# Scores with the query stationary, and packed by column tile, in a decode attention kernel

## Chip, cores and metric

The kernel runs on one core of a Trainium2 chip. The metric is device time in microseconds (us) of one execution; lower is better. A kernel's time is the median of several executions. A program on one core has no second core to compare with, so "fast" here only means that a run lies within 1.5% of the fastest of the same kernel.

PE is the matmul engine (PEld its weight loads), DVE the vector engine, ACT the scalar engine, POOL the general engine, SP the engine that issues the DMAs. "The Trainium skill" is a set of notes on the chip, named by page title and section.

## The reference, cut to what matters

One token of a decoder block: layer norm, attention over a long cache, and a small feed-forward block. Nearly all the data is the cache.

```python
x: (1, 1, 448)   Hq, Hkv, Sk, Dh = 16, 8, 32768, 256        # all bf16
k_cache, v_cache: (1, 8, 32768, 256)                        # 134 MB each
scores = einsum("bhqd,bhkd->bhqk", q, k) * Dh**-0.5         # 2 query heads share a K/V head
p = softmax(scores, axis=-1)
o = einsum("bhqk,bhkd->bhqd", p, v)
h = x + o @ wo;   h2 = h + FFN(layernorm(h))                # FFN: 448 -> 1792 -> 448, Mish
```

K and V together are 268.4 MB. The other weights are about 10 MB.

## The kernel before

The cache is read in chunks of 4096 rows (2 MiB): 8 chunks of K and 8 of V for each of 8 K/V heads ("groups"). Chunks share six rotating SBUF buffers. While the K chunks of group g come in, so do the V chunks of group g−1. K is transposed on PE, two bf16 at a time as one f32; the copy out of PSUM is called an eviction here.

```python
    for b in range(NB):                                   # k_chunk: 8 batches of 4 slabs of 128 rows
        pst = ps_t.tile([P, 4, P], F32, ...)
        for jj in range(4):
            nc.tensor.transpose(out=pst[:, jj, :], in_=kn[:, j, :].bitcast(F32), identity=ident_f[:])
        kT = ktp.tile([P, 4, P, 2], BF16, ...)            # evicted by ACT (3 of 8) or DVE (5 of 8)
        ...
        for jj in range(4):
            for e in range(2):                            # kT is the weight, q (2 columns padded to 16) moves
                nc.tensor.matmul(out=pss[:, j, :], lhsT=kT[:, jj, :, e], rhs=qT_pad[:, g, e, :], ...)
    # ... softmax_group: DVE max, POOL all-reduce of the max, two exps on ACT, sum by a matmul
    # v_chunk: 16 matmuls of 512 columns in four column tiles
            nc.tensor.matmul(out=acc[32 * t:32 * t + 2 * REP, reg, :], lhsT=pT[:, slab:slab + 2, :]...,
                             rhs=vn[:, j:j + 2, :]..., tile_position=(0, 32 * t))
```

The tile pools are laid out in SBUF in the order in which they are opened: first small constants, then small work tiles, then the six stream buffers:

```python
    const = ctx.enter_context(tc.tile_pool(name="const", bufs=1))
    small = ctx.enter_context(tc.tile_pool(name="small", bufs=2))
    stream = ctx.enter_context(tc.tile_pool(name="stream", bufs=STREAM_BUFS))   # kn and vn
```

So every byte in `const` and `small` moves the buffers into which K and V land.

## Time and profile before

| | before |
|---|---|
| median, fastest, slowest of the first 5 runs | 683.9, 683.62, 684.43 us |
| profiled span | 682.2 us |
| K/V transfers | 128 of 2 MiB |
| share of the span that the 16 DMA engines were busy with queue q1 | 97.4% |
| PE / DVE / ACT busy | 81% / 38% / 31% |

The first fence is from the page of the kernel before: busy time by engine, then rows of 40 equal slices of the span (a digit is a busy share in tenths, the last row is what the DMA engines moved), then the DMA queues with packets, MB, and the time of their packets as a share of 16 engines' span.

```profile
PE 549.6 (81%) x7643; PEld 418.6 (61%) x7643; DVE 256.3 (38%) x475; ACT 208.7 (31%) x231; POOL 11.8 (2%) x29
...
DMA  8999999999999999999999999999999999999981
GB/s 282 399 427 425 427 422 413 427 426 422 426 424 429 424 427 426 427 425 426 426 426 428 426 425 428 425 427 426 423 427 428 424 426 427 428 424 426 428 366 61
...
q1 hardware_dynamic: 22090, 279.00, 97.4%
q8 instruction: 60, 0.98, 0.6%
```

The DMA engines never rest, and the rate sits near 426 GB/s from the third slice to the 38th. That is the bound. Besides the data, the same engines carry 60 packets of 16 KiB that bring instructions.

The second fence is from the groups of instructions of the kernel before: line, engine, operation, tiles, shapes, count; then busy us and mean ns; then the idle time before them and what ended it.

```profile
L209 PE MATMUL pst<-ident_f,kn 128*128 128x128 f32 x2048 | 353.3, 306 | 44.2 <-DMA kn<-in_A_k_cache_dram 44.2
L215 DVE COPY kT<-pst 128x512 f32<-128x512 f32 x320 | 221.0, 691 | 290.4 <-PE pst L209 288.9
L212 ACT COPY kT<-pst 128x1024 bf16<-128x1024 bf16 x192 | 194.2, 1011 | 398.3 <-PE pst L209 393.2
L220 PE MATMUL pss<-qT_pad,kT 128*128 128x16 bf16 x4096 | 184.0, 172 | 22.7 <-DVE kT L215 17.0
L255 PE MATMUL acc<-vn,pT 128*4 128x512 bf16 x1024 | 101.9, 422 | 14.4 <-DMA vn<-in_A_v_cache_dram 14.4
```

PE waits for K data (44.2 us in front of the transposes), not the data for PE. The P·V matmuls (L255) last 422 ns each but cover 101.9 us in all, 100 ns each: about four overlap.

### The profile page before, as it was taken

To read this page: it belongs to the slowest core of one execution; us is meant where nothing else is said; L and a number is where in the kernel's file an instruction comes from. 1 tells how busy PE (TensorE), PEld (TensorE's weight loads), DVE (VectorE), ACT (ScalarE), POOL (GpSimd) and SP (SyncE) were. 2 spreads that over 40 slices of the span, in tenths; PEclk is the share of its full clock that TensorE was granted. 3 is DMA by queue.
4 is the path that set the end of the run, shared out by engine and by line. 5 is a ranking of instruction groups with operands and counts; after the bars stand their busy time and mean duration, and the time that the engine had idled before them with its cause. 6 is when DMAs were issued, how large, how long until landed. Compare 5 with 4: busy or idle time off the path is not lost.

```text
span 682.2 us, 16927 instructions
## 1 busy us (share of the span) xinstructions
PE 549.6 (81%) x7643; PEld 418.6 (61%) x7643; DVE 256.3 (38%) x475; ACT 208.7 (31%) x231; POOL 11.8 (2%) x29
## 2 busy tenths in 40 slices
PE   2869979987998897888887789888988979877345
PEld 2757756666765775666566666567656757665114
DVE  1335624442443443343433334334433334434002
ACT  0324443332332342232332234222332323322101
POOL 2100000000000000000000000000000000000000
PEclk9969979997998888987998789877899889889655
DMA  8999999999999999999999999999999999999981
GB/s 282 399 427 425 427 422 413 427 426 422 426 424 429 424 427 426 427 425 426 426 426 428 426 425 428 425 427 426 423 427 428 424 426 427 428 424 426 428 366 61
DMA packets 22164, 280.08 MB, mean 411 GB/s; under 512 B 2186, under 2 KB 4235, under 8 KB 5580
## 3 DMA queue, kind: packets, MB, share of 16 engines
q1 hardware_dynamic: 22090, 279.00, 97.4%
q8 instruction: 60, 0.98, 0.6%
q14 instruction: 12, 0.10, 0.0%
q10 hardware_dynamic: 2, 0.00, 0.0%
HBM read 278.99 MB, written 0.00 MB: 409 GB/s over the span
## 4 chain that ended last, share of the span: by engine, by line
DMA 41%; PE 38%; issue 9%; DVE 5%; ACT 4%; POOLq 1%; POOL 1%; SPq 0%; ACTq 0%; DVEq 0%
DMA kn<-in_A_k_cache_dram 36%; PE pst L209 20%; PE pss L220 10%; PE acc L255 6%; DMA vn<-in_A_v_cache_dram 3%; DVE kT L215 3%; ACT kT L212 3%; DMA wq_sb<-in_A_wq_dram 2%; POOLq L367 1%; ACT pT L236 1%; DVE m L228 1%; PE psm L162 1%; PE psm L310 1%; POOL mall L230 0%; DVE S L222 0%
## 5 line engine op out<-in xcount | busy, mean ns | idle before, releaser
L209 PE MATMUL pst<-ident_f,kn 128*128 128x128 f32 x2048 | 353.3, 306 | 44.2 <-DMA kn<-in_A_k_cache_dram 44.2
L215 DVE COPY kT<-pst 128x512 f32<-128x512 f32 x320 | 221.0, 691 | 290.4 <-PE pst L209 288.9
L212 ACT COPY kT<-pst 128x1024 bf16<-128x1024 bf16 x192 | 194.2, 1011 | 398.3 <-PE pst L209 393.2
L209 PEld LDWEIGHTS pst<-ident_f,kn 128*128 128x128 f32 x2048 | 246.9, 155 | 68.8 <-issue 45.4
L220 PEld LDWEIGHTS <-kT 128*128 128x128 bf16 x4096 | 156.6, 99 | 98.7 <-DVE kT L215 51.4
L220 PE MATMUL pss<-qT_pad,kT 128*128 128x16 bf16 x4096 | 184.0, 172 | 22.7 <-DVE kT L215 17.0
L255 PE MATMUL acc<-vn,pT 128*4 128x512 bf16 x1024 | 101.9, 422 | 14.4 <-DMA vn<-in_A_v_cache_dram 14.4
L255 PEld LDWEIGHTS <-pT 128*4 128x4 bf16 x1024 | 20.2, 85 | 37.4 <-issue 33.7
L222 DVE COPY S<-pss 128x64 f32<-128x64 f32 x64 | 14.4, 224 | 44.5 <-PE pss L220 44.5
L239 PE MATMUL psm<-L,ones_f 128*128 128x2 f32 x16 | 3.7, 300 | 21.0 <-ACT pT L236 20.9
L239 PEld LDWEIGHTS psm<-L,ones_f 128*128 128x128 f32 x16 | 3.0, 234 | 22.6 <-ACT pT L236 22.6
L236 ACT ACTIVATE pT<-S,negM 128x256 bf16<-128x256 f32 x16 | 8.8, 575 | 23.3 <-POOL negM L231 22.8
L264 DVE COPY accn<-acc 128x512 f32<-128x512 f32 x8 | 5.5, 682 | 27.7 <-PE acc L255 27.7
L267 PE MATMUL psm<-sel,accn 128*128 128x2 f32 x32 | 7.0, 287 | 9.0 <-DVE accn L264 9.0
L267 PEld LDWEIGHTS psm<-sel,accn 128*128 128x128 f32 x32 | 5.9, 229 | 13.4 <-DVE accn L264 13.4
L141 ACT ACTIVATE rstd_ln<-psm,eps_t 128x1 f32<-128x1 f32 x2 | 0.5, 261 | 42.4 <-PE psm L139 42.4
L230 POOL PARTITION_ALL_REDUCE mall<-m x8 | 3.0, 376 | 540.5 <-DVE m L228 540.5
L241 DVE RECIPROCAL rl<-psm 128x2 f32<-128x2 f32 x8 | 1.3, 169 | 20.3 <-PE psm L239 20.3
L280 PEld LDWEIGHTS <-wo_flat 128*128 128x128 bf16 x128 | 5.5, 108 | 3.0 <-issue 3.0
L269 PE MATMUL psm<-sel,accn 128*128 128x2 f32 x32 | 7.1, 292 | 0.0
L162 PE MATMUL psm<-cenbf_ln,wq_sb 128*128 128x1 bf16 x128 | 3.7, 165 | 3.7 <-DMA wq_sb<-in_A_wq_dram 3.3
L280 PE MATMUL psm<-oT,wo_flat 128*128 128x1 bf16 x128 | 4.4, 164 | 2.5 <-DVE oT L273 2.5
(71 smaller groups left out, 61.3 us busy)
## 6 DMA issues: line engine op xcount, KB each, us to landing
kn<-in_A_k_cache_dram SPq DMA_DIRECT2D x64, 2048.0 KB, 21.8
vn<-in_A_v_cache_dram SPq DMA_DIRECT2D x64, 2048.0 KB, 24.5
wo_flat<-in_A_wo_dram SPq DMA_DIRECT2D x1, 3584.0 KB
wq_sb<-in_A_wq_dram SPq DMA_DIRECT2D x2, 1536.0 KB, 9.4
w_flat<-in_B_w_dram SPq DMA_DIRECT2D x1, 1568.0 KB, 30.0
w_sb<-in_B_w_dram SPq DMA_DIRECT2D x1, 1344.0 KB, 26.8
wq_sb<-in_A_wq_dram SPq DMA_DIRECT2D x2, 256.0 KB, 11.8
w_sb<-in_B_w_dram SPq DMA_DIRECT2D x1, 224.0 KB
```

Of the source, the lines that this page charges most:

```text
L162: nc.tensor.matmul(out=psm[:, PM_Q + fb:PM_Q + fb + 1], lhsT=wq_sb[:, c, h * DH:(h + 1) * DH].rearrange("p (i e) -> p e i", e=2)[:, e, :], ...
L209: nc.tensor.transpose(out=pst[:, jj, :], in_=kn[:, j, :].bitcast(F32), identity=ident_f[:])
L212: nc.scalar.copy(out=kT[:].rearrange("p a r e -> p (a r e)"), in_=pst[:].rearrange("p a r -> p (a r)").bitcast(BF16))
L215: nc.vector.tensor_copy(out=kT[:].rearrange("p a r e -> p (a r e)").bitcast(F32), in_=pst[:].rearrange("p a r -> p (a r)"))
L220: nc.tensor.matmul(out=pss[:, j, :], lhsT=kT[:, jj, :, e], rhs=qT_pad[:, g, e, :], start=(e == 0), stop=(e == 1))
L222: nc.vector.tensor_copy(out=S_sb[:, c * J:(c + 1) * J, :], in_=pss[:, :, 0:REP])
L228: nc.vector.tensor_reduce(out=m1[:], in_=view, axis=AX.X, op=ALU.max)
L236: nc.scalar.activation(out=pT[:, :, hh], in_=view[:, hh, :], func=ACT.Exp, bias=negM[:, h:h + 1], scale=SCALE, accum_out=L1[:, h:h + 1])
L255: nc.tensor.matmul(out=acc[32 * t:32 * t + 2 * REP, reg, :], lhsT=pT[:, slab:slab + 2, :].rearrange("p s h -> p (s h)"), rhs=vn[:, j:j + 2 ...
L267: nc.tensor.matmul(out=psm[:, PM_OT + dc * REP:PM_OT + (dc + 1) * REP], lhsT=accv[:, 0, dc, :], rhs=sel32[:, 0:REP], start=True, stop=False)
L269: nc.tensor.matmul(out=psm[:, PM_OT + dc * REP:PM_OT + (dc + 1) * REP], lhsT=accv[:, 1, dc, :], rhs=sel32[:, REP:2 * REP], start=False, st ...
L280: nc.tensor.matmul(out=psm[:, PM_ATT + nb:PM_ATT + nb + 1], lhsT=wo_flat[:, col * D + nb * P:col * D + (nb + 1) * P], rhs=oT[:, dc, hh:hh ...
```

## The change

Intent: take work off PE. The scores are turned round, so that q (two columns) is the weight and 512 K positions move, four column tiles at once: 16 matmuls a chunk instead of 64. The scores come out as rows (each of the four column tiles fills two partitions, one a query head, so 8 of 128 partitions carry scores), so they must be transposed back before P·V (8 small transposes a chunk). Evictions are split evenly between ACT and DVE, ACT copies 512 f32 instead of 1024 bf16, and the softmax sum is now combined over the partitions by POOL, as the maximum was before.

```diff
-EVAC_ON_ACT = (False, True, False, False, True, False, True, False)
+EVAC_ON_ACT = (False, True, False, True, False, True, False, True)
-KT_BUFS = 8
+KT_BUFS = 7
...
-    ones_f = const.tile([P, P], F32, name="ones_f")
...
-    b1_row = const.tile([1, FF], BF16, name="b1_row")          # moves to the pool of wq, behind the stream
...
-            for jj in range(4):
-                for e in range(2):
-                    nc.tensor.matmul(out=pss[:, j, :], lhsT=kT[:, jj, :, e], rhs=qT_pad[:, g, e, :],
-                                     start=(e == 0), stop=(e == 1))
-        nc.vector.tensor_copy(out=S_sb[:, c * J:(c + 1) * J, :], in_=pss[:, :, 0:REP])
+            for e in range(2):
+                for t in range(4):
+                    kT = kTs[bg * 4 + t]
+                    nc.tensor.matmul(out=bank[32 * t:32 * t + REP, :], lhsT=qT2[:, g, e, :],
+                                     rhs=kT[:, :, :, e], start=(e == 0), stop=(e == 1),
+                                     tile_position=(0, 32 * t))
+            nc.vector.tensor_scalar(out=S1[:, col0:col0 + 512], in0=bank[:], scalar1=1.0, scalar2=None,
+                                    op0=ALU.mult, op1=ALU.max, accum_out=rmax[:, idx:idx + 1])
...
+        for c in range(NCH):                                    # softmax_exp, once a group
+            nc.scalar.activation(out=S1[:, c * CCOLS:(c + 1) * CCOLS], ..., func=ACT.Exp, ...)
...
+        for blk in range(NB):                                   # p_transpose, once a chunk
+            nc.tensor.transpose(out=ppt[:, blk, :], in_=S1[:, col0:col0 + P], identity=ident_bf[:])
```

Which transfers are issued, in which order, and into how many buffers, does not change. (Cuts in the code are marked with three dots; the comments in the diffs are mine.) In the compiled program the six stream buffers start at byte 29376 of each partition (and every 16384 behind it) before, and at 25344 after. PE has 13181 instructions before and 8083 after.

More of the change, by code (lines that the diff above doesn't have):

```diff
@@ L16 @@
 P = 128
-EVAC_ON_ACT = (False, True, False, False, True, False, True, False)
+EVAC_ON_ACT = (False, True, False, True, False, True, False, True)
+S_EVAC_ON_ACT = (False, False)
 J_SLABS = 32
 STREAM_BUFS = 6
-KT_BUFS = 8
-S_PAD = 16
-PV_TILES = 4
+KT_BUFS = 7
+S_LAG = 2
+NEG_BIG = -3.0e38
 @with_exitstack
@@ L54 @@
     J = J_SLABS
+    assert J == 32
     CH = J * P
     NCH = SK // CH
-    assert SK % CH == 0 and J % 4 == 0
-    NCJ = NCH * J
+    assert SK % CH == 0
     SCALE = float(DH) ** -0.5
@@ L61 @@
     NB = J // 4
+    NHALF = 2
+    CCOLS = NHALF * 512
+    NCOLS = NCH * CCOLS
     const = ctx.enter_context(tc.tile_pool(name="const", bufs=1))
@@ L66 @@
     ktp = ctx.enter_context(tc.tile_pool(name="ktp", bufs=KT_BUFS))
+    s1p = ctx.enter_context(tc.tile_pool(name="s1p", bufs=2))
     ptp = ctx.enter_context(tc.tile_pool(name="ptp", bufs=2))
-    ssp = ctx.enter_context(tc.tile_pool(name="ssp", bufs=2))
     ps_t = ctx.enter_context(tc.tile_pool(name="ps_t", bufs=3, space=bass.MemoryType.PSUM))
-    ps_s = ctx.enter_context(tc.tile_pool(name="ps_s", bufs=2, space=bass.MemoryType.PSUM))
+    ps_s = ctx.enter_context(tc.tile_pool(name="ps_s", bufs=1, space=bass.MemoryType.PSUM))
+    ps_p = ctx.enter_context(tc.tile_pool(name="ps_p", bufs=1, space=bass.MemoryType.PSUM))
     ps_a = ctx.enter_context(tc.tile_pool(name="ps_a", bufs=1, space=bass.MemoryType.PSUM))
@@ L77 @@
     make_identity(nc, ident_f[:])
-    ones_f = const.tile([P, P], F32, name="ones_f")
-    nc.vector.memset(ones_f[:], 1.0)
     onesD = const.tile([P, P], F32, name="onesD")
@@ L90 @@
     nc.vector.tensor_reduce(out=sel32[:], in_=ident_f[:].rearrange("p (t q) -> p q t", q=32), axis=AX.X, op=ALU.add)
+    sel2 = sel32[:, 0:REP]
+    selneg2 = const.tile([P, REP], F32, name="selneg2")
+    nc.vector.tensor_scalar(out=selneg2[:], in0=sel2, scalar1=-SCALE, scalar2=None, op0=ALU.mult)
+    negbig2 = const.tile([P, REP], F32, name="negbig2")
+    nc.vector.tensor_scalar(out=negbig2[:], in0=sel2, scalar1=-NEG_BIG, scalar2=NEG_BIG, op0=ALU.mult, op1=ALU.add)
     psm = ps_m.tile([P, 512], F32, name="psm")
-    acc = ps_a.tile([P, 2, 2 * DH], F32, name="acc")
+    acc = ps_a.tile([P, 2 * DH], F32, name="acc")
     nc.vector.memset(acc[:], 0.0)
+    pss = [ps_s.tile([P, 512], F32, name=f"pss{i}") for i in range(2)]
+    for i in range(2):
+        nc.vector.memset(pss[i][:], 0.0)
     PM_X = 0
@@ L98 @@
     PM_VAR = 8
-    PM_L = 10
     PM_OT = 12
@@ L110 @@
     nc.sync.dma_start(out=x_row[0:1, 0:D], in_=A_x[0, 0:1, :])
-    b1_row = const.tile([1, FF], BF16, name="b1_row")
-    nc.sync.dma_start(out=b1_row[0:1, :], in_=B_b1.rearrange("(o f) -> o f", o=1))
     wq_pool = tc.tile_pool(name="wq", bufs=1)
     wqp = wq_pool.__enter__()
+    b1_row = wqp.tile([1, FF], BF16, name="b1_row")
+    nc.sync.dma_start(out=b1_row[0:1, :], in_=B_b1.rearrange("(o f) -> o f", o=1))
     wq_sb = wqp.tile([P, NDC, HQ * DH], BF16, name="wq_sb")
@@ L164 @@
                                  rhs=cen1_bf[:, c:c + 1], start=(c == 0), stop=(c == NDC - 1))
-    qT_pad = const.tile([P, HKV, 2, S_PAD], BF16, name="qT_pad")
-    nc.gpsimd.memset(qT_pad[:], 0.0)
-    nc.vector.tensor_scalar(out=qT_pad[:, :, :, 0:REP].rearrange("p g e hh -> p g hh e"),
+    qT2 = const.tile([P, HKV, 2, REP], BF16, name="qT2")
+    nc.vector.tensor_scalar(out=qT2[:].rearrange("p g e hh -> p g hh e"),
                             in0=psm[:, PM_Q:PM_Q + NFB].rearrange("p (g hh e) -> p g hh e", g=HKV, hh=REP),
@@ L187, in load_ffn_weights, with flush_pending @@
         nc.sync.dma_start(out=w2_flat[:, 0:NFC * D], in_=B_w2.rearrange("(p fc) n -> p (fc n)", p=P))
-    L1 = const.tile([P, HQ], F32, name="L1")
-    negM = const.tile([P, HQ], F32, name="negM")
-    rl = const.tile([P, HQ], F32, name="rl")
     attn_sb = const.tile([P, NDC], F32, name="attn_sb")
     nc.vector.memset(attn_sb[:], 0.0)
-    S_tiles = {}
+    S1_tiles = {}
+    rmax_tiles = {}
     pT_tiles = {}
+    rl_tiles = {}
+    sbank = [0]
+    pending = []
+    def flush_pending():
+        while pending:
+            pending.pop(0)()
     def k_chunk(g, c):
@@ L201, in k_chunk, with scores @@
         if c == 0:
-            S_tiles[g] = ssp.tile([P, NCJ, REP], F32, name=f"S_{g}", tag="S")
-        S_sb = S_tiles[g]
-        pss = ps_s.tile([P, J, S_PAD], F32, name=f"pss_{g}_{c}", tag="pss")
+            S1_tiles[g] = s1p.tile([P, NCOLS], BF16, name=f"S1_{g}", tag="S1")
+            rmax_tiles[g] = small.tile([P, NCH * NHALF], F32, name=f"rmax_{g}", tag="rmax")
+        S1 = S1_tiles[g]
+        rmax = rmax_tiles[g]
+        kTs = {}
+        def scores(bg):
+            bank = pss[sbank[0] % 2]
+            sbank[0] += 1
+            for e in range(2):
[4 more added lines that the diff above has]
+                                     tile_position=(0, 32 * t))
+            col0 = (c * NHALF + bg) * 512
+            idx = c * NHALF + bg
+            nc.vector.tensor_scalar(out=S1[:, col0:col0 + 512], in0=bank[:], scalar1=1.0, scalar2=None,
+                                    op0=ALU.mult, op1=ALU.max, accum_out=rmax[:, idx:idx + 1])
         for b in range(NB):
@@ L211, in k_chunk @@
             if EVAC_ON_ACT[b % 8]:
-                nc.scalar.copy(out=kT[:].rearrange("p a r e -> p (a r e)"),
-                               in_=pst[:].rearrange("p a r -> p (a r)").bitcast(BF16))
+                nc.scalar.copy(out=kT[:].rearrange("p a r e -> p (a r e)").bitcast(F32),
+                               in_=pst[:].rearrange("p a r -> p (a r)"))
             else:
@@ L216, in k_chunk @@
                                       in_=pst[:].rearrange("p a r -> p (a r)"))
-            for jj in range(4):
-                j = b * 4 + jj
-                for e in range(2):
-                    nc.tensor.matmul(out=pss[:, j, :], lhsT=kT[:, jj, :, e], rhs=qT_pad[:, g, e, :],
-                                     start=(e == 0), stop=(e == 1))
-        nc.vector.tensor_copy(out=S_sb[:, c * J:(c + 1) * J, :], in_=pss[:, :, 0:REP])
-    def softmax_group(g):
-        S_sb = S_tiles.pop(g)
-        view = S_sb[:].rearrange("p cj hh -> p hh cj")
-        m1 = small.tile([P, REP], F32, name=f"m1_{g}", tag="m1")
-        nc.vector.tensor_reduce(out=m1[:], in_=view, axis=AX.X, op=ALU.max)
-        mall = small.tile([P, REP], F32, name=f"mall_{g}", tag="mall")
-        nc.gpsimd.partition_all_reduce(out_ap=mall[:], in_ap=m1[:], channels=P, reduce_op=ReduceOp.max)
-        nc.gpsimd.tensor_scalar(out=negM[:, g * REP:(g + 1) * REP], in0=mall[:], scalar1=-SCALE, scalar2=None,
-                                op0=ALU.mult)
-        pT = ptp.tile([P, NCJ, REP], BF16, name=f"pT_{g}", tag="pT")
-        for hh in range(REP):
-            h = g * REP + hh
-            nc.scalar.activation(out=pT[:, :, hh], in_=view[:, hh, :], func=ACT.Exp, bias=negM[:, h:h + 1],
-                                 scale=SCALE, accum_out=L1[:, h:h + 1])
-        pT_tiles[g] = pT
-        nc.tensor.matmul(out=psm[:, PM_L:PM_L + REP], lhsT=ones_f[:], rhs=L1[:, g * REP:(g + 1) * REP],
-                         start=True, stop=True)
-        nc.vector.reciprocal(out=rl[:, g * REP:(g + 1) * REP], in_=psm[:, PM_L:PM_L + REP])
@@ new lines, in k_chunk, with softmax_stats @@
+            kTs[b] = kT
+            if b == S_LAG - 1:
+                flush_pending()
+            if b - S_LAG == 3:
+                scores(0)
+        pending.append(lambda: scores(1))
+    def softmax_stats(g):
+        rmax = rmax_tiles.pop(g)
+        rowmax = small.tile([P, 1], F32, name=f"rowmax_{g}", tag="rowmax")
+        nc.vector.tensor_reduce(out=rowmax[:], in_=rmax[:], axis=AX.X, op=ALU.max)
+        m2 = small.tile([P, REP], F32, name=f"m2_{g}", tag="m2")
+        nc.vector.scalar_tensor_tensor(out=m2[:], in0=sel2, scalar=rowmax[:, 0:1], in1=negbig2[:],
+                                       op0=ALU.mult, op1=ALU.add)
+        mall = small.tile([P, REP], F32, name=f"mall_{g}", tag="mall")
+        nc.gpsimd.partition_all_reduce(out_ap=mall[:], in_ap=m2[:], channels=P, reduce_op=ReduceOp.max)
+        junk2 = small.tile([P, REP], F32, name=f"junk2_{g}", tag="junk2")
+        negM_row = small.tile([P, 1], F32, name=f"negM_{g}", tag="negM")
+        nc.vector.scalar_tensor_tensor(out=junk2[:], in0=mall[:], scalar=1.0, in1=selneg2[:],
+                                       op0=ALU.mult, op1=ALU.mult, accum_out=negM_row[:])
+        return negM_row
@@ new lines, in softmax_exp @@
+    def softmax_exp(g, negM_row):
+        S1 = S1_tiles[g]
+        lrow = small.tile([P, NCH], F32, name=f"lrow_{g}", tag="lrow")
+        for c in range(NCH):
+            nc.scalar.activation(out=S1[:, c * CCOLS:(c + 1) * CCOLS], in_=S1[:, c * CCOLS:(c + 1) * CCOLS],
+                                 func=ACT.Exp, bias=negM_row[:, 0:1], scale=SCALE, accum_out=lrow[:, c:c + 1])
+        lsum = small.tile([P, 1], F32, name=f"lsum_{g}", tag="lsum")
+        nc.vector.tensor_reduce(out=lsum[:], in_=lrow[:], axis=AX.X, op=ALU.add)
+        l2 = small.tile([P, REP], F32, name=f"l2_{g}", tag="l2")
+        nc.vector.tensor_scalar(out=l2[:], in0=sel2, scalar1=lsum[:, 0:1], scalar2=None, op0=ALU.mult)
+        lall = small.tile([P, REP], F32, name=f"lall_{g}", tag="lall")
+        nc.gpsimd.partition_all_reduce(out_ap=lall[:], in_ap=l2[:], channels=P, reduce_op=ReduceOp.add)
+        rl = small.tile([P, REP], F32, name=f"rl_{g}", tag="rl")
+        nc.vector.reciprocal(out=rl[:], in_=lall[:])
+        rl_tiles[g] = rl
+        pT_tiles[g] = ptp.tile([P, NCH, J, REP], BF16, name=f"pT_{g}", tag="pT")
@@ new lines, in p_transpose @@
+    def p_transpose(g, c):
+        S1 = S1_tiles[g]
+        pT = pT_tiles[g]
+        ppt = ps_p.tile([P, NB, P], BF16, name=f"ppt_{g}_{c}", tag="ppt")
+        for blk in range(NB):
+            col0 = c * CCOLS + blk * P
+            nc.tensor.transpose(out=ppt[:, blk, :], in_=S1[:, col0:col0 + P], identity=ident_bf[:])
+        for bg in range(NHALF):
+            nc.vector.tensor_copy(
+                out=pT[:, c, bg * 16:(bg + 1) * 16, :].rearrange("p (t jj) hh -> p jj t hh", t=4),
+                in_=ppt[:, bg * 4:(bg + 1) * 4, :].rearrange("p jj (t q) -> p jj t q", q=32)[:, :, :, 0:REP])
@@ L245, in v_chunk @@
         nc.sync.dma_start(out=vn[:], in_=A_v_cache[0, g, c * CH:(c + 1) * CH, :].rearrange("(r j) d -> r j d", j=J))
+        if c + 1 < NCH:
+            p_transpose(g, c + 1)
         pT = pT_tiles[g]
-        reg = g % 2
         NPAIR = J // 2
         for pi in range(NPAIR):
-            t = pi % PV_TILES
+            t = pi % 4
             j = 2 * pi
-            slab = c * J + j
-            first = (c == 0 and pi < PV_TILES)
-            last = (c == NCH - 1 and pi >= NPAIR - PV_TILES)
-            nc.tensor.matmul(out=acc[32 * t:32 * t + 2 * REP, reg, :],
-                             lhsT=pT[:, slab:slab + 2, :].rearrange("p s h -> p (s h)"),
+            first = (c == 0 and pi < 4)
+            last = (c == NCH - 1 and pi >= NPAIR - 4)
+            nc.tensor.matmul(out=acc[32 * t:32 * t + 2 * REP, :],
+                             lhsT=pT[:, c, j:j + 2, :].rearrange("p s h -> p (s h)"),
                              rhs=vn[:, j:j + 2, :].rearrange("p a d -> p (a d)"),
@@ L261, in finish_group @@
         pT_tiles.pop(g)
-        reg = g % 2
+        S1_tiles.pop(g)
+        rl = rl_tiles.pop(g)
         accn = small.tile([P, 2 * DH], F32, name=f"accn_{g}", tag="accn")
-        nc.vector.tensor_copy(out=accn[:], in_=acc[:, reg, :])
+        nc.vector.tensor_copy(out=accn[:], in_=acc[:])
         accv = accn[:].rearrange("p (s i e) -> p s e i", s=2, e=2)
@@ L273, in finish_group @@
             nc.vector.tensor_tensor(out=oT[:, dc, :], in0=psm[:, PM_OT + dc * REP:PM_OT + (dc + 1) * REP],
-                                    in1=rl[:, g * REP:(g + 1) * REP], op=ALU.mult)
+                                    in1=rl[:], op=ALU.mult)
         for nb in range(NDC):
@@ L287, in finish_group, with softmax_group @@
                                 in1=attn_sb[0:DLAST, NDC - 1:NDC], op=ALU.add)
+    def softmax_group(g):
+        flush_pending()
+        negM_row = softmax_stats(g)
+        softmax_exp(g, negM_row)
+        p_transpose(g, 0)
     for c in range(NCH):
```

## The prediction

> **What bounds the kernel now.** The K and V stream. Every 8 us stretch from 40 to 656 us moves 417 to 432 GB/s with the DMA engines fully busy, except 96 to 112 us (404 and 414; windows view). The DMA table: 128 transfers of 2 MiB, q1 97.4% of 16 engines. One transfer lasts 2.097 MB / 426 GB/s = 4.92 us, so a K/V pair takes 9.85 us. With a backlog PE does a pair in 7.85 us (timeline, 112.5 to 120.4 us), then waits for K data (44 us in all, groups view), and the queue is about 22 us ahead of it (issue to landing 21.8 us). After the last V chunk lands (663.8 us) a serial tail of 18.4 us follows.
>
> **What the change removes, adds and moves.**
> - Scores: 4096 matmuls with kT stationary (184.0 us in all, 2.9 us a chunk) become 16 matmuls a chunk of 512 columns with two query columns stationary, in four column tiles. The 1024 P·V matmuls have that form already: mean 422 ns, but they cover only 101.9 us, 0.1 us each. So I estimate 1.6 us a chunk. The Trainium skill, "TensorE: Matmul & The Clock Gate", Part 3, says that matmuls in different column tiles run concurrently; this trace agrees (422 against 100 ns).
> - ACT evictions: 3 of 1011 ns a chunk become 4 on 512 f32 elements, an estimated 0.6 us each.
> - DVE a chunk: 5 copies of 0.69 us + 0.22 become 4 × 0.69, two score evictions (estimate 0.7 us each) and two small copies (0.15 us each): 3.7 us to about 4.5 us.
> - Added: 8 bf16 transposes a chunk (about 0.6 us of PE), and eight 1024-wide exps a group in place of two 256-wide (0.58 us each): about 8 to 10 us of ACT a group against 1.2 us. The second all-reduce feeds only the normalisation.
> - A pair: PE about 7 to 7.5 us, DVE 4.5, ACT 3.5. All below 9.85 us. DMA bytes, stream buffers and transfer order are unchanged.
>
> **Critical path.** Almost none. Weak spots are the group boundaries: maximum to exp is 8 to 11.5 us already (POOL all-reduce, chain of waits); the change lengthens it by the deferred scores, the first exp and the transposes (2 to 4 us), and the exps may hold up ACT evictions for several us. PE may fall 10 us further behind; the queue's 22 us lead should absorb that, and each pair regains over 2 us. In the first, K-only group PE took 6.56 us a chunk against 4.92; about 5.2 us now should remove the 96 to 112 us dip, worth 0.6 us. The tail is untouched.
>
> **Prediction.** 683.3 us, range 681.0 to 686.5. Faster by over 2%: 1%. Within 2%: 95%. Slower: 4%.
>
> **What would show it.** Right: DMA again about 426 GB/s in nearly all slices; PE busy share lower (about 70%), its idle time before the K transposes, released by DMA, over 44 us; scores covering about 100 us; last V landing near 663 us; a tail of 18 us. Wrong at a step: score matmuls covering over 200 us; slices below 415 GB/s just after a boundary; idle PE there released by ACT for over 20 us.
>
> **What would make it wrong.** The strided read of kT as moving operand halves the matmul rate and PE passes 9.85 us a pair; or the boundaries stall PE beyond the 22 us lead, so the stream stops eight times.

## The result, and the profile after

674.96 us (674.22 to 675.58, 7 runs) against 683.9 us: ratio 0.9868, 95% interval 0.9858 to 0.9878. Ratios are the mean time of one kernel's fast runs over that of the other's of the same rounds, so not quite the ratio of the medians quoted. The gain is 9 us, 1.3%: inside "within 2%", but below the predicted range.

The lines of the page after that answer to those above:

```profile
PE 516.4 (77%) x5067; PEld 359.4 (53%) x5067; DVE 301.2 (45%) x774; ACT 227.8 (34%) x391; POOL 12.5 (2%) x28
...
DMA  8999999999999999999999999999999999999992
GB/s 282 418 425 432 429 430 430 429 430 430 430 430 427 430 432 430 427 433 431 427 432 426 431 431 427 431 430 428 432 426 432 430 428 431 429 431 429 430 390 74
...
q1 hardware_dynamic: 22090, 279.00, 97.9%
q8 instruction: 40, 0.66, 0.3%
```

And the groups after:

```profile
L240 PE MATMUL pst<-ident_f,kn 128*128 128x128 f32 x2048 | 303.2, 305 | 78.2 <-DMA kn<-in_A_k_cache_dram 76.2
L243 ACT COPY kT<-pst 128x512 f32<-128x512 f32 x256 | 149.3, 586 | 359.1 <-PE pst L240 355.8
L233 DVE TENSOR_SCALAR_CACHE_REDUCE S<-pss 128x512 bf16<-128x512 f32 x128 | 88.4, 691 | 84.0 <-PE pss L228 84.0
L228 PE MATMUL pss<-kT,qT 128*2 128x512 bf16 x1024 | 112.7, 393 | 1.1
L274 ACT ACTIVATE S<-S,negM 128x1024 bf16<-128x1024 bf16 x64 | 72.6, 1135 | 28.1 <-DVE junk L266 28.1
```

The engines did what the change meant: scores cover 112.7 us instead of 184.0, and PE waits longer for K data (76.2 us instead of 44.2). That wait is the saved PE time turned into waiting. It gained nothing by itself. What changed is a row that no engine sets: the rate, about 430 GB/s in nearly every slice instead of about 426, with the DMA engines fully busy both times.

Where the 9 us lie is read from the last P·V matmuls in the timeline. Before:

```profile
663.78 1.88 PE L255 MATMUL acc<-vn,pT 128*4 128x512 bf16 x16 [3.02 <-DMA vn<-in_A_v_cache_dram]
```

After:

```profile
654.56 1.88 PE L311 MATMUL acc<-vn,pT 128*4 128x512 bf16 x16 [3.67 <-DMA vn<-in_A_v_cache_dram]
```

The last chunk lands 9.2 us earlier; the tail behind it is the same, 18.4 us (682.15 − 663.78 and 672.92 − 654.56). So the whole gain is in the stream, and it builds up over the whole run: the last landing of a chunk is 2.5 us earlier at the 19th chunk, 6.5 at the 78th and 9.6 at the 123rd of 128.

A finer look at the trace's record of single DMA packets (a K/V packet is 16 KiB, the part of a chunk that goes to one partition; 1024 of them fall to each of the 16 engines):

```
                                         before     after
most common packet durations, ns         613, 620   611
mean over all 16384 packets, ns          618.2      613.6
instruction packets on q8, mean ns       60, 1071   40, 938
```

Two things differ, then: most packets take 2 to 9 ns longer before, and there are 20 instruction packets more. A second record, the moments at which the 16 engines report their share of one chunk as landed, shows what such a packet does. These are the 16 landings of one late chunk (the 123rd of 128; the last one at 639.1 us before and at 629.5 us after), in us behind the first:

```
before  0.0 0.2 1.2 1.3 1.5 1.6 2.2 5.2 9.7 9.7 9.8 9.8 9.8 10.0 11.0 11.2
after   0.0 0.1 0.1 0.2 0.4 1.0 2.8 5.4 5.5 5.7 7.0 7.2 7.2  7.2  7.3  7.4
```

Early in the run the spread is 2 us in both. The engines drift apart, and about nine of them run late. A chunk is complete only when the last of them is done, so the late engines set the end of the stream.

### The profile page after: what moved, and what is told of

The parts are those of the page before. It is cut to its first block, busy times and chain, and to the rows that moved or that the text cites. A ratio compares the mean times of both kernels' runs of the same rounds, so it can differ in the third digit from the quotient of the medians.

```text
span 672.9 us, 12241 instructions
## 1 busy us (share of the span) xinstructions
PE 516.4 (77%) x5067; PEld 359.4 (53%) x5067; DVE 301.2 (45%) x774; ACT 227.8 (34%) x391; POOL 12.5 (2%) x28
## 4 chain that ended last, share of the span: by engine, by line
DMA 46%; PE 37%; ACT 7%; DVE 5%; issue 4%; POOL 1%; POOLq 0%; SPq 0%
DMA kn<-in_A_k_cache_dram 43%; PE pst L240 22%; ACT S L274 7%; PE pss L228 6%; DMA vn<-in_A_v_cache_dram 3%; PE ppt L293 3%; PE acc L311 3%; DVE S L233 1%; DVE pT L295 1%; DVE accn L321 1%; PE psm L324 1%; PE psm L326 1%; PE psm L172 1%; PE psm L373 1%; ACT kT L243 0%
## 5 line engine op out<-in xcount | busy, mean ns | idle before, releaser
L240 PE MATMUL pst<-ident_f,kn 128*128 128x128 f32 x2048 | 303.2, 305 | 78.2 <-DMA kn<-in_A_k_cache_dram 76.2
L243 ACT COPY kT<-pst 128x512 f32<-128x512 f32 x256 | 149.3, 586 | 359.1 <-PE pst L240 355.8
L246 DVE COPY kT<-pst 128x512 f32<-128x512 f32 x256 | 176.8, 691 | 158.3 <-PE pst L240 145.7
L233 DVE TENSOR_SCALAR_CACHE_REDUCE S<-pss 128x512 bf16<-128x512 f32 x128 | 88.4, 691 | 84.0 <-PE pss L228 84.0
L228 PE MATMUL pss<-kT,qT 128*2 128x512 bf16 x1024 | 112.7, 393 | 1.1
L311 PE MATMUL acc<-vn,pT 128*4 128x512 bf16 x1024 | 79.0, 397 | 15.6 <-DMA vn<-in_A_v_cache_dram 15.3
L274 ACT ACTIVATE S<-S,negM 128x1024 bf16<-128x1024 bf16 x64 | 72.6, 1135 | 28.1 <-DVE junk L266 28.1
L293 PE MATMUL ppt<-ident_bf,S 128*128 128x128 bf16 x512 | 46.1, 239 | 33.0 <-DVE pT L295 17.8
L293 PEld LDWEIGHTS <-S 128*128 128x128 bf16 x512 | 34.1, 106 | 47.6 <-ACT S L274 23.9
L228 PEld LDWEIGHTS <-qT 128*2 128x2 bf16 x1024 | 23.7, 81 | 44.7 <-issue 32.9
L233 DVE DVE_READ_ACCUMULATOR S<-pss 128x1 f32 x128 | 10.6, 83 | 0.0
```

Of the source, the lines that this page charges most:

```text
L228: nc.tensor.matmul(out=bank[32 * t:32 * t + REP, :], lhsT=qT2[:, g, e, :], rhs=kT[:, :, :, e], start=(e == 0), stop=(e == 1), tile_positio ...
L233: nc.vector.tensor_scalar(out=S1[:, col0:col0 + 512], in0=bank[:], scalar1=1.0, scalar2=None, op0=ALU.mult, op1=ALU.max, accum_out=rmax[:, ...
L243: nc.scalar.copy(out=kT[:].rearrange("p a r e -> p (a r e)").bitcast(F32), in_=pst[:].rearrange("p a r -> p (a r)"))
L246: nc.vector.tensor_copy(out=kT[:].rearrange("p a r e -> p (a r e)").bitcast(F32), in_=pst[:].rearrange("p a r -> p (a r)"))
L274: nc.scalar.activation(out=S1[:, c * CCOLS:(c + 1) * CCOLS], in_=S1[:, c * CCOLS:(c + 1) * CCOLS], func=ACT.Exp, bias=negM_row[:, 0:1], sc ...
L293: nc.tensor.transpose(out=ppt[:, blk, :], in_=S1[:, col0:col0 + P], identity=ident_bf[:])
```

## The experiments

Theory A (placement): a K/V destination that does not start on a multiple of 256 bytes costs each packet some ns. Theory B (instruction packets): PE's instructions come over the same DMA engines, and fewer instructions hold them up less. Theory C (PE's work): less PE work and SBUF traffic by the new score form lets the stream run faster. In the expectations B' and B'' are later forms of B, and D is a later form of C. All kernels ran five rounds, beside the kernel before on the same chip; its median there was 684.1 to 684.6, so times from different rounds compare to some 0.5 us. Runs marked "wrong on purpose" do less arithmetic. The comparison with the reference still passed them (presumably because the attention output is small beside the residual; not checked), so "correct" proves nothing for them, and little for the other kernels.

### Placement: pads in both directions

```diff
     # before, in front of the stream buffers (after_pad: 192, 128 or 32 bytes the same way)
+    pad_t = const.tile([P, 16], F32, name="pad_t")       # 64 bytes a partition
+    nc.vector.memset(pad_t[:], 0.0)
```

> The kernel before with 64 unused bytes in front of the stream tiles, so that every K/V destination starts at a multiple of 256 bytes (29440) as in the changed kernel (25344), not at 192 above one (29376). Theory A (placement of the destination): 16 KiB packets fall from 613 to 620 ns to a uniform 611 ns, the stream rate rises from about 426 to about 429 GB/s, and the time falls by 3.5 to 5 us, to about 679.5. Theory B (fewer PE instructions, so fewer instruction fetches on the DMA engines) and theory C (less SBUF traffic by the new scores): no change, 683.9 within 1, packets as before.

Measured: 678.32 us, ratio 0.9916 (0.9902 to 0.9929). Sixty-four unused bytes take 5.7 us off the kernel before. Of its 16384 packets, 16003 now take 611 ns.

The control has the same pad in a pool of its own between the stream buffers and everything behind them:

> Control: the same 64 bytes placed behind the stream tiles, so that kT, pT, S and the weights move but the K/V destinations stay at 29376. Theory A: no change, 683.9 within 1, packets 613 to 620 ns. If instead the placement of the tiles that the engines read mattered, it would gain what the other pad gains.

Measured: 682.95 us, ratio 0.9986 (0.9973 to 1.0): a gain of about 1 us (interval 0 to 1.8), and packets of 613 and 620 ns as before. So it is not the tiles that the engines read, except perhaps for this 1 us. Against its control the front pad gains 4.6 us.

The traces show where that 1 us arises. In the kernel before the stream dips at 96 to 112 us, just behind the first group; with the front pad it hardly does, though PE takes 6.57 us for a K chunk of the first group in both. The lines give the window, its length, the busy time of PE, PEld, DVE, ACT and POOL, the granted PE clock, the DMA share, and GB/s; the kernel before first, then with 64 bytes:

```profile
96.00:104.00 8.00, 7.53 (x111) 6.18 (x109) 3.67 (x6) 3.04 (x3) 0.00 (x0) 0.88 1.01 404
104.00:112.00 8.00, 7.61 (x118) 5.62 (x115) 3.68 (x6) 3.04 (x3) 0.00 (x0) 1.00 0.98 414
```

```profile
96.00:104.00 8.00, 7.17 (x121) 5.58 (x119) 3.49 (x7) 3.04 (x3) 0.00 (x0) 1.00 1.00 423
104.00:112.00 8.00, 7.60 (x116) 5.62 (x115) 3.83 (x7) 3.04 (x3) 0.00 (x0) 1.00 1.01 430
```

In the control these windows read 421 and 424 GB/s, and its lead of 1.2 us over the kernel before is there by the 19th chunk and does not grow. Why the dip is smaller in both padded kernels stays open.

The opposite pad in the changed kernel:

> The changed kernel with 192 unused bytes in front of the stream tiles: K/V destinations at 25536, 192 above a multiple of 256, as in the kernel before. Theory A: packets go to 613 to 620 ns, the rate from 430 to about 426 GB/s, the time up by 3.5 to 5 us, to about 679. Theories B and C: no change, 675 within 1.

Measured: 680.62 us, 5.7 us slower than the changed kernel; packets 613 and 620 ns. The rates of the two padded kernels, first the kernel before with 64 bytes, then the changed one with 192:

```profile
GB/s 295 414 432 428 427 431 429 428 426 426 430 428 429 424 430 425 430 428 433 427 429 428 429 430 428 430 428 428 427 428 429 428 432 426 429 428 433 410 380 59
```

```profile
GB/s 251 399 430 428 422 429 426 426 425 428 427 425 428 424 427 429 428 422 428 428 427 424 428 426 427 427 425 427 427 427 423 429 429 416 425 429 427 425 390 76
```

From the third slice to the 38th the mean is 428.1 and 426.3 GB/s, against 425.6 in the kernel before and 429.6 in the changed one. Both padded kernels sit between: each has one part of the cause.

Which step matters?

> The changed kernel with 128 unused bytes in front: destinations at 25472, a multiple of 128 but not of 256. If the step that matters is 128 bytes or less: no change, packets 611, 675. If it is 256: packets 613 to 620 ns and 678 to 681, as with 192.

Measured: 680.37 us; a quarter of the packets still takes 611 ns, the others mostly 612 to 619 (mean 617.3). So 128 bytes are not enough.

> The changed kernel with 32 unused bytes in front: destinations at 25376, a multiple of 32 but not of 64. Theory A: at least as slow as with 192, 680 to 690; packets 613 ns or longer.

Measured: 681.85 us; packets mostly 614 and 621 ns (mean 618.4).

What follows: with starts that are multiples of 256 almost all packets took 611 ns (16003 and 16211 of 16384), and all other starts tried (32, 128, 192 above one) gave more on average. The Trainium skill, "DMA: Bandwidth & Descriptors", section "How a descriptor splits into AXI transactions", says that transactions of 256 bytes must start at multiples of 256 and that a descriptor that does not is split with extra beats. It states this for what is read; these runs show a step at the same 256 bytes on the side that is written, with 2 to 10 ns on a packet of 611. By the means, the longer packets account for 3.0 us in the kernel before (3.0 ns times 1024 packets an engine) and for 4.2 us of 5.7 in the changed one (4.1 ns). Of the 5.7 us that the front pad took off the kernel before, 1 us came with the control too; the rest, 1 to 2 us in either kernel, was not resolved. Theory A is shown for 4.6 us (against the control) to 5.7 us (against the kernel before) of the 9. The skill's "SBUF — State Buffer", section "Who interferes with whom", says that DMA never contends with a compute engine. The control does not test this, since it moves the engines' tiles and leaves their work; the nearest test is b64_pvhalf below, where 14 us less PE work gained 0.8 us, so no run here shows it cleanly.

### The other 3.4 us: instruction packets?

The padded kernel before (678.3) and the changed kernel (675.0) have the same most common packet duration, 611 ns (means 615.3 and 613.6), and still differ by 3.4 us. The Trainium skill, "Runtime: NRT & Kernel Launch", section "Instruction fetch mechanics", says that instructions come in 16 KiB blocks of 256, and calls the cost mostly hidden. The count agrees: 13181 − 8083 PE instructions are 19.9 blocks, and q8 falls from 60 to 40. Whether the cost is hidden from PE was not looked at; from the DMA engine it is not: a block takes 0.94 us (changed kernel) to 1.07 us (kernel before) on average, and in the padded kernel before 57 of the 60 blocks overlap in time with a data packet that takes about 1.1 us instead of 0.61; at random times only 2 or 3 of 60 would. Summed over the 16 landings of a chunk, the lag behind the fastest engine grew by 92 us over 53 fetches in the padded kernel before and by 53 us over 35 in the changed one: 1.7 and 1.5 us a fetch. The growth comes with the fetches: from one chunk to the next whose landings can be told apart (the 22nd to the 126th), the sum grows by 0.1 us on average where no fetch falls between their late landings (the mean of the last nine; 36 gaps in the changed kernel, 23 in the padded one), and by 1.5 and 1.75 us where one does (28 and 38 gaps).

First attempts to move the number of fetches:

```diff
+        if c < NCH - 1:                                          # a_fetch, in k_chunk
+            for _ in range(92):
+                nc.gpsimd.memset(fetch_pad[0:1, 0:1], 0.0)
...
+        for _ in range(40):                                      # a_pe40 (a_pe20: 20), in v_chunk
+            nc.tensor.matmul(out=psm[0:4, 300:301], lhsT=ident_bf[:, 0:4], rhs=ident_bf[:, 0:1],
+                             start=True, stop=True)
```

> The changed kernel with 5152 one-element memsets on the otherwise idle POOL (destinations still 256 above a multiple of 512), which brings the instruction-fetch packets back from 40 to about 60. Theory B (fetches): the time rises by 2 to 5 us. Theory A: at most 1 us, since 20 packets of about 0.6 us of engine time over 16 engines are 0.8 us.

Measured: 993 us. A miss, and useless for this question, since q8 stayed at 40 packets: the memsets took 89 ns each, 459 us of POOL, in front of the all-reduce that every group waits for, and the stream stopped at every group boundary:

```profile
GB/s 318 413 429 406 1 85 365 429 391 1 0 295 429 430 202 0 1 314 425 431 186 0 0 306 431 430 189 0 0 316 429 429 430 431 430 428 429 432 430 180
...
q8 instruction: 40, 0.66, 0.2%
q14 instruction: 56, 0.46, 0.1%
```

It shows two things by accident: what a boundary that outlasts the queue's lead looks like, and that POOL's instructions are fetched on another queue (q14, 15 packets in the changed kernel, 56 here).

> The changed kernel with 40 tiny unused matmuls (and their weight loads) after the P·V matmuls of each V chunk: 5120 PE instructions more, as many PE instructions as the kernel before has, so that the 16 KiB instruction-fetch packets on queue q8 go from 40 back to about 60. Destinations stay at 25344. Theory B' (the 3.4 us that placement does not explain are instruction fetches sharing the DMA engines): fetch packets 60, time up by 2.5 to 3.5 us to about 678. Rival D (they come from the new score form itself, less waiting and less traffic by PE): time up by less than 1 us, even though fetches rise to 60.

Measured: 695.11 us, 20 us more, with 60 fetches. Confounded by starvation: the matmuls took so much of PE (85% busy) that the stream ran dry at boundaries, which the rate shows (349, 315, 374):

```profile
GB/s 267 416 428 430 429 349 406 429 431 425 315 428 431 427 404 374 434 426 431 408 425 432 427 431 365 428 431 428 405 415 433 427 430 351 428 431 429 427 420 113
...
q8 instruction: 60, 0.98, 0.5%
```

> Half the dose, 20 tiny matmuls a V chunk: about 50 fetch packets. Theory B': up by 1.2 to 1.8 us, to about 676.5. Rival D: less than 0.7 us.

Measured: 677.12 us (676.27 to 679.03), 2.2 more, 50 fetches. That fits theory B', but two slices of its profile (391 and 416 GB/s) show the stream starved for about 2 us in the profiled run, so it proves nothing.

Then fewer instructions, wrong on purpose:

```diff
-            for e in range(2):                                   # less: half of the score matmuls
+            for e in range(1):
...
-        for pi in range(NPAIR):                                  # less: 4 of 16 P.V matmuls
+        for pi in range(4):
```

> Wrong result on purpose: the changed kernel with half of the score matmuls and a quarter of the P·V matmuls, 2560 PE instructions fewer, so about 30 fetch packets instead of 40. Same transfers, same destinations. From the landing spread of the earlier runs (about half of the 16 engines run late; 20 fetches more made them some 4 us later) theory B' gives 0.17 us a fetch: 1.7 us less than 675.0, about 673.3. Its pair is less_fill20.

Measured: 675.74 us, 0.8 more than the changed kernel, where 1.7 less was expected. A miss.

> Wrong on purpose: as the run less, plus 20 tiny matmuls a V chunk, which put the 2560 PE instructions back (about 40 fetches) while PE does less work than in the changed kernel. Theory B': back to 675.0, 1.2 to 2.2 us over less. Rival D (the time follows PE's work, not its instruction count): within 0.5 us of less.

Measured: 673.97 us, 1.8 less than its pair, where 1.2 to 2.2 more was expected. A miss in the wrong direction. Theory D does not explain it either: the kernel with more PE work was faster.

> Wrong on purpose: as less, plus 60 tiny matmuls a V chunk: as many PE instructions as the kernel before, about 60 fetches, without the boundary stalls that spoilt a_pe40. Theory B': 30 fetches over less, 4 to 6 us over it, about 678.5, and the spread of one chunk's landings over the 16 engines again near 11 us at the end. Rival D: within 1 us of less.

Measured: 699.9 us (693.94 to 704.89), starved at boundaries like a_pe40.

The landings show part of why `less` and its pair went wrong. Late landings of one chunk, in us behind the first:

```
less          0.0 0.1 1.0 1.2 1.7 1.7 4.3 4.3 4.4 4.5 4.6 5.6 5.6 5.7 5.8 7.9
less_fill20   0.0 0.0 0.1 0.2 0.2 0.6 0.9 3.3 4.2 4.3 4.4 4.6 4.6 4.6 4.7 4.9
```

In `less` the group of late engines is at 5.8 us, 1.6 less than in the changed kernel (10 fetches fewer: as expected), but one single engine lags 2.1 us behind all others, and the stream ends with it. In `less_fill20` the stream ran short for a moment (one slice at 406 GB/s), the queue drained, the engines came level, and the spread began anew from 3 us. But the two traces differ from the first chunk on, before any filler has run: its last landing is at 22.8 us in `less` and at 19.2 us in `less_fill20`, and `less` is 2.1 us behind at the 32nd chunk (184.0 against 182.0 us) and at the 64th (341.2 against 339.1). So most of the difference between these two traces arose in the first loads, for a reason that no run tested, and this pair says little about fetches. What it suggests is that the end of the stream follows not the count of fetches but the lag of the slowest engine. That is theory B'': fetches fall in turn on about half of the engines, and the last engine decides.

Theory B'' was tried in the kernel whose schedule does not starve, the padded kernel before:

```diff
-                for e in range(2):                               # b64_half: one of two score matmuls
-                    nc.tensor.matmul(out=pss[:, j, :], lhsT=kT[:, jj, :, e], rhs=qT_pad[:, g, e, :],
-                                     start=(e == 0), stop=(e == 1))
+                nc.tensor.matmul(out=pss[:, j, :], lhsT=kT[:, jj, :, 0], rhs=qT_pad[:, g, 0, :],
+                                 start=True, stop=True)
+                # b64_half_fill: and a tiny matmul of 4 weight columns and 1 moving column
```

> Wrong result on purpose: the kernel before, with the 64-byte pad (678.3), and only the first of the two score matmuls of each slab: 4096 PE instructions fewer, about 44 fetch packets instead of 60, the same transfers, evictions and softmax. Theory B'' (a fetch holds one DMA engine up by about 1.4 us; only about half of the engines get them, in turn, and the stream ends with the most delayed engine): 16 fetches fewer over about 8 engines are 2 turns, 2.9 us: 675.4, and the spread of a late chunk's 16 landings falls from 11.6 to 8 or 9 us. If PE's instruction count has nothing to do with it: 678.3.

Measured: 675.21 us, 3.1 less, with 44 fetches; the late spread is 9.2 us instead of 11.7. This hit the expected 675.4. (One of its six runs took 681.76; it is counted in the ratio, 0.9880, interval 0.9853 to 0.9908.) By itself it does not separate the theories, since PE had less work too.

> Wrong on purpose, the pair of b64_half: the second score matmul is replaced, in place, by a tiny unused matmul (4 columns of weights, 1 column moving), so the instruction count (about 60 fetches) is that of the padded kernel before, and PE does less work than there. Theory B'': 678.3 again, 2 to 4 us over b64_half, spread near 11 us. Rival D (PE's work or SBUF traffic): like b64_half within 0.7 us.

Measured: 684.94 us, with dips to 306 GB/s: starved again, and of no use as a pair.

> The changed kernel with 50 tiny unused matmuls after V chunks 3 to 6 of each group only, away from the group boundaries: 3200 PE instructions more, about 52 fetches instead of 40. Theory B'': 1.5 turns, 1.4 to 2.9 us over 675.0, 676.4 to 677.9, and a late spread of about 9 us instead of 7.4, if no slice shows the DMA starved. Otherwise 675.

Measured: 681.62 us, but with three slices at 386 to 388 GB/s inside the stream: starved too, in spite of the choice of chunks.

Refilling a kernel with tiny matmuls never gave a clean test. The last pair therefore took away PE work and left the instructions:

```diff
-                             rhs=vn[:, j:j + 2, :].rearrange("p a d -> p (a d)"),   # 512 columns
+                             rhs=vn[:, j, :],                                        # 256 columns
```

> Wrong result on purpose: the kernel before, with the 64-byte pad (678.3), every P·V matmul with 256 moving columns instead of 512: the same PE instructions (60 fetches), some 40 to 50 us less PE busy time, about as much as b64_half took away. Theory B'': 678.3 within 1, and the late spread of the 16 landings stays near 11.6 us. Rival D (PE's work): 675 to 676, like b64_half.

Measured: 677.51 us, 0.8 less; spread 10.7 us. PE busy time fell by 14 us (543.7 to 529.7), not by the 40 to 50 that was expected, so it is a weaker test than planned: b64_half took 29 us of PE and 3.1 us of time.

> Wrong on purpose: the same in the changed kernel (40 fetches). Theory B'': 675.0 within 1, spread near 7.4 us. Rival D: 672 to 673.

Measured: 674.73 us, 0.2 less; spread 8.1 us. PE busy time fell by 14 us as well.

The busy lines and instruction packets of the two padded kernels, first b64_half, then b64_pvhalf:

```profile
PE 514.8 (76%) x5595; PEld 376.6 (56%) x5595; DVE 256.3 (38%) x476; ACT 208.1 (31%) x231; POOL 11.8 (2%) x29
...
q8 instruction: 44, 0.72, 0.4%
```

```profile
PE 529.7 (78%) x7643; PEld 436.0 (65%) x7643; DVE 256.5 (38%) x476; ACT 208.6 (31%) x231; POOL 11.8 (2%) x29
...
q8 instruction: 60, 0.98, 0.5%
```

What follows for the 3.4 us: the two causes can be told apart in the four kernels with and without pad, by when the fastest and the slowest of the 16 engines land the same chunk, the third from the end (in us from the start):

```
starts, instruction packets                fastest   slowest   apart
kernel before: not on 256, 60               642.6     653.8     11.3
kernel before, 64 bytes: on 256, 60         636.3     648.0     11.7
changed, 192 bytes: not on 256, 40          643.6     650.7      7.1
changed: on 256, 40                         636.7     644.1      7.4
```

The start of the buffers moves the fastest engine by 6 to 7 us and leaves the spread; two kernels with the same start have fastest engines within 1 us of each other and differ in the spread, by about 4 us, which is the size of the missing time. The spread grows fetch by fetch in each trace, as said above. Taking 16 fetches away gave the predicted 3.1 us; taking PE work away without them gave 0.8 and 0.2, and left the spread near its old value (10.7 and 8.1 us). Against it stands that no run that added fetches was clean, that `less` gained nothing, with a late start that was not controlled, and that the separating pair was weak. So that a fetch delays single engines is shown in the traces; that theory B'' is the whole of the 3.4 us is supported, not proven, and up to 1 us of PE's own share isn't excluded.

### A trial to beat both

```diff
+        if g == HKV - 1 and 2 <= c < NCH - 1:                    # v_chunk, last group
+            for _ in range(30):
+                nc.tensor.matmul(out=psm[0:4, 256:512], lhsT=ident_bf[:, 0:4], rhs=vn[:, 0, :],
+                                 start=True, stop=True)
```

> A trial to beat both: the changed kernel with 30 unused matmuls of 256 columns after each of V chunks 2 to 6 of the last group, so that PE is not idle between the last chunks and its granted clock stays up for the serial tail (0.50 there now). If the clock holds: last P·V group 1.0 us instead of 1.9 and the tail 2 to 4 us shorter, 671 to 673. If it does not hold: 675, one fetch more.

Measured: 672.98 us (672.55 to 673.25), ratio 0.9833 (0.9821 to 0.9846): 2 us faster than the changed kernel, with the correct computation. The Trainium skill, "TensorE: Matmul & The Clock Gate", Part 1, says that PE's clock halves after some 3.4 us of idleness. The last V chunks are 4.9 us apart, and in the changed kernel PE ran the last P·V group in 1.88 us at a granted clock of 0.50. Here that clock is 1.00 (windows view), and, from the timeline:

```profile
654.47 1.03 PE L311 MATMUL acc<-vn,pT 128*4 128x512 bf16 x16 [0.59 <-DMA vn<-in_A_v_cache_dram]
...
661.08 3.47 PE L377 MATMUL psm<-cenbf_ln,w_sb 128*128 128x1 bf16 x56 [0.35 <-ACT rstd_ln L151]
```

The group takes 1.03 us, but 7 us into the tail, at a granted clock of 0.50 again, the longest step (L377) takes 3.47 us as before (3.48): the tail itself leaves PE idle again. The stream ended at the same time as in the changed kernel (654.47 against 654.56), so this gain is one of the tail alone.

## Why the prediction was right or wrong

- **The bound.** Right: the stream bounds both kernels, and its engines are busy throughout in both.
- **The work of the engines.** Nearly right. Scores 112.7 us for "about 100"; ACT evictions 586 ns for 0.6 us; score evictions 691 ns for 0.7; exps 1.135 us plus 0.187 for reading the sum, 10.6 us a group for "8 to 10"; small transposes 46.1 us, 0.72 us a chunk for 0.6. PE is 77% busy, not 70%. The Trainium skill's concurrency of column tiles holds for the scores as well: 393 ns each, 112.7 us / 1024 = 110 ns in the sum.
- **Boundaries.** Right: no slice below 415 GB/s after one. PE did wait there for ACT (13.8 us before the small transposes), under the stated 20.
- **The first group.** The dip at 96 to 112 us is gone as said, but not for the stated reason alone. A K chunk took 5.83 us there (in the timeline its transposes start at 54.66, 60.48, 66.31 and 72.14 us), not 5.2, so PE still fell behind the stream; and the dip is nearly gone (423 and 430 GB/s) in the padded kernel before, where PE takes the old 6.57 us. The hit was partly luck.
- **The tail.** Right: 18.4 us.
- **The step that failed.** It is "One transfer lasts 2.097 MB / 426 GB/s = 4.92 us", carried over to the changed kernel with "DMA bytes, stream buffers and transfer order are unchanged". The 426 GB/s was read from the profile and then taken for a property of the chip. It was a property of this kernel: of where its buffers start (4.6 to 5.7 us) and, as far as the runs show, of its instruction packets (most of 3.4 us). At 430 GB/s one transfer lasts 4.88 us, and the 268.4 MB take 5.9 us less than at 426 GB/s, before any lag of single engines. The stated bytes were not unchanged either: the q8 line, 60 packets, stood on the page before, and the diff's smaller PE program meant 20 packets fewer; and the stream buffers, as many as before, no longer started at the same bytes.
- **The sentence that gave 1% to a large gain** was still sound: the gain was 1.3%. Only the range was too narrow, since every term of the sum was charged to an engine and none to the stream.

## What to carry to other kernels

When a kernel is bound by DMA, a change of the compute engines can still move the time, through what it does to the DMA engines: look at where destination tiles start (a multiple of 256 bytes here, worth 0.7 to 0.8% for 64 bytes of padding) and at the instruction packets on the queues. Never carry a measured rate over to a changed kernel before asking what set it. And watch the spread of the 16 landings of one chunk: a stream ends with its slowest engine, and mean rates hide that.

## What the Trainium skill lacked or had wrong

- "DMA: Bandwidth & Descriptors" gives the 256-byte rule for reads; it lacks that an SBUF destination off a multiple of 256 costs time too: mostly 613 to 621 ns against 611 a 16 KiB packet, 4.6 to 5.7 us of 684 in this kernel.
- "Runtime: NRT & Kernel Launch" calls instruction fetch mostly hidden; it lacks that a fetch of 16 KiB holds one data DMA engine up by about 1.5 to 1.7 us, and that the slowest engine is late by 7 us (40 fetches) to 11 us (60 fetches) at the end of a 640 us stream.
- "DMA: Bandwidth & Descriptors", section "Where 436 GB/s comes from", says that the HBM side, at about 358 GB/s, binds HBM to SBUF transfers; these streams ran at 426 to 430 GB/s on one core. The same page's measured table has 425 GB/s for a core alone, and these runs agree with that.
- No page says that POOL's instructions come as 8 KiB packets on a queue other than PE's (q14, 0.12 MB in 15 packets in the changed kernel, 0.46 MB in 56 with 5152 more POOL instructions). Whether other engines share q14 was not tested.
